# An mLSTM cell and a gated feed-forward layer: two batches of attention at a time from the third chunk on, the PSUM pool of the products split, half of the new states beside the values

## The chip, the cores and the metric

The kernel runs on one core of one Trainium2 chip. The time is the device time of one execution, in microseconds (us). A core has a matrix engine (TensorE, PE in the profile, its weight loads PEld), a vector engine (VectorE, DVE), a scalar engine (ScalarE, ACT), GpSimd (POOL) and SyncE (SP), which issues the transfers here. Each engine takes its own queue of instructions in order and waits on semaphores for the others. Results of TensorE go to PSUM, which has 8 banks; everything else works from SBUF.

## What is computed

For 4 batches and 8 heads, over 768 time steps with 40 elements per head, the reference runs a recurrent cell and feeds its output to a feed-forward layer, all in float32:

```python
for t in range(S):
    m_new = np.maximum(f_gate[:, :, t] + m, i_gate[:, :, t])
    f_stab = np.exp(f_gate[:, :, t] + m - m_new)
    i_stab = np.exp(i_gate[:, :, t] - m_new)
    m = m_new
    C = f_stab[:, :, None, None] * C + i_stab[:, :, None, None] * np.einsum('bhd,bhe->bhde', vt, kt)
    n = f_stab[:, :, None] * n + i_stab[:, :, None] * kt
    h_tilde = np.einsum('bhde,bhe->bhd', C, qt)
    nq = np.einsum('bhd,bhd->bh', n, qt)[:, :, None]
    denom = np.maximum(np.abs(nq), 1.0)
    y[:, :, t] = 1.0 / (1.0 + np.exp(-o_gate[:, :, t])) * h_tilde / denom
x = y as (batch*time, head*40)              # 3072 x 320
h = x @ w_in                                # 320 -> 2048
out = (h * (1.0 / (1.0 + np.exp(-1.702 * h)))) @ w_out   # 2048 -> 320
```

## The kernel before

**Tiling.** Time is cut into six chunks of 128 steps (chunk 0 to 5, `w` in the code). Within a chunk the recurrence becomes attention: a 128x128 matrix of weights per head from the gates, times the scores of queries and keys, times the values, plus the queries times the state that the chunks before left. At the end of a chunk the state (one 40x41 block per head) is scaled and the chunk's own sum is added. A chunk has 4 batches x 128 steps = 512 tokens, which are the columns of the feed-forward layer.

**Functions, one per step.** `columns` transposes the gate sums to columns (`p_cols`). `weights(w, b)` turns batch `b`'s row of gate sums into weights: eight exponentials on ScalarE (line 330), then a mask on GpSimd (line 333). `scores(w, b)` makes eight 40-row products of queries and keys in two PSUM tiles (`p_s`, line 343) and multiplies them into the weights on VectorE (two instructions at line 345). `values(w, b)` makes the products with the values (`p_o`, line 354) and with the state (`p_i`, line 360), then VectorE runs a chain of seven instructions (lines 364 to 374) that ends in `y`, and GpSimd copies a 64-column tail of it (line 376). `seam(w, b)` transposes `y` on TensorE (`p_x`, line 383); ScalarE copies it to `xT`. `scale(w, b)` scales the values and the old state on GpSimd (lines 390 and 394). `carry(w)` makes the chunk's sums in two halves of 16 heads (`p_c`, line 403) and adds them to the state on VectorE (line 407). `transposes(w, b)` transposes queries and keys on VectorE (line 298).

`up(w, j, n)` is the first layer (`p_h`, lines 429 and 435) with the activation on ScalarE (line 440). The second layer is `down` for chunk 0 (four accumulators of 320 columns, 16 blocks), and `down_fast` for the others: 14 blocks of eight matmuls (`p_out`, line 530), seven for each pair of batches, in a scheme that needs seven products in place of eight and sums of hidden columns and of weights (`hidden_sums`, lines 511 to 515, on VectorE). Behind each block, VectorE copies or adds its accumulator into the output tile (lines 533 and 535); blocks 5 and 6, and 12 and 13, end with the store of one batch's rows.

**Order.** The order on each engine is the order of the calls (a manual schedule); semaphores follow from tiles and pools. Chunk w+1's attention is laid among chunk w's down blocks: `attention(w + 1)` returns a list of steps, and behind each block whose number is in `stops` the next step is run. Before, a step holds one function each of up to four batches: the weights of batch s, the scores of batch s-1, the values of s-2, the seam of s-3. `carry` runs early in the next chunk's `up`.

**PSUM.** Two pools of four banks: `ps_a` (tag "a": columns, scores, values, states, seams, and half of an `up`'s hidden tiles) and `ps_m` (tag "m": the other half of the hidden tiles and all `p_out`). A tile takes the next bank of its pool in turn; its first matmul waits until what was in the bank has been read.

```python
elif w + 2 < NW and i == 0:
    load_gates(w + 2)
    load_blocks(w + 2)
block()
if i in stops and side:
    run(side.pop(0))
```

Of the kernel before, what the change touches and what calls it, by code (L numbers as in the profile page):

```python
# [8 lines left out]
FP = mybir.dt.float32  # L9
# [5 lines left out]
PSUM = bass.MemoryType.PSUM  # L15
# [7 lines left out]
L = 128  # L23
# [11 lines left out]
def kernel(  # L35
# [13 lines left out]
    B, H, S, D = q.shape  # L49
    BH = B * H  # L50
    DM = H * D
    DFF = moe_w_in.shape[1]
    NW = S // L
    NP = H // 2
    NF = DFF // 128
    D1 = D + 1
# [12 lines left out]
    op = ctx.enter_context(tc.tile_pool(name="op", bufs=2))  # L69
    rows = ctx.enter_context(tc.tile_pool(name="rows", bufs=2, space=bass.MemoryType.DRAM))  # L70
    ps_a = ctx.enter_context(tc.tile_pool(name="ps_a", bufs=4, space=PSUM))
    ps_m = ctx.enter_context(tc.tile_pool(name="ps_m", bufs=4, space=PSUM))
    ctx.enter_context(tc.manual_schedule())

    V, A, G, T = nc.vector, nc.scalar, nc.gpsimd, nc.tensor
# [9 lines left out]
    v_st = const.tile([L, BH, D1], FP, name="v_st")  # L85
# [130 lines left out]
    kT, qT, wt, ys, xT, gs, o_ps, sums = {}, {}, {}, {}, {}, {}, {}, {}  # L216
# [119 lines left out]
            A.activation(out=eo[w], in_=eo[w], func=AF.Tanh, scale=0.5)  # L336

    def scores(w, b):
        pw = [ps_a.tile([L, NP, L], FP, tag="a", name="p_s") for _ in range(2)]
        for p in range(NP):  # L340
            for i in range(2):
                r = slice(i * 64, i * 64 + D)
                T.matmul(pw[i][:, p, :], kT[w, b][r, p, :], qT[w, b][r, p, :], start=True, stop=True)  # L343
        for i in range(2):
            V.tensor_tensor(out=wt[w, b][:, :, i, :], in0=pw[i], in1=wt[w, b][:, :, i, :], op=OP.mult)  # L345
# [47 lines left out]
            old = state[:, b * NP:(b + 1) * NP].rearrange("p j a b -> p j (a b)")  # L393
            G.tensor_tensor(out=old, in0=old, in1=d, op=OP.mult)

    def carry(w):
        for c in range(2):
            ps = slice(c * 2 * NP, (c + 1) * 2 * NP)
            pc = ps_a.tile([128, 2 * NP, D1], FP, tag="a", name="p_c")
            for p in range(2 * NP):  # L400
                for i in range(2):
                    h = c * 4 * NP + 2 * p + i
                    T.matmul(pc[i * 64:i * 64 + D, p, :], k_st[:, h, 0:D], v_st[:, h, :], start=True, stop=True)  # L403
            for i in range(2):
                r = slice(i * 64, i * 64 + D)
                if w:
                    V.tensor_tensor(out=state[r, ps, i, :], in0=pc[r], in1=state[r, ps, i, :], op=OP.add)
                else:
                    V.tensor_copy(out=state[r, ps, i, :], in_=pc[r])
        G.memset(v_st[:, :, D:D1], 1.0)  # L410


    def up(w, j, n, between=None, states=False):

        x = xT[w].rearrange("p c b t -> p c (b t)")
        begin, end = range(j, j + n // 2), range(j + n // 2, j + n)
        ph = {}
        ts = slice(0, W)  # L420

        def take(j, pool, tag):
            ph[j] = [pool.tile([128, W], FP, tag=tag, name="p_h") for _ in range(2)]

        def full(j, first):
            for c in range(2):
                for i in range(2):
                    f = 2 * j + i
                    T.matmul(ph[j][i][:, ts], w_in_sb[:, c, f * 128:(f + 1) * 128], x[:, c, ts],  # L429
                             start=(first and c == 0), stop=(not first and c == 1))  # L430

        def rest(j, first):
            for i in range(2):
                r = slice(i * 64, i * 64 + 64)
                T.matmul(ph[j][i][:, ts], w_in_x[r, j, :], x[r, 2, ts], start=first, stop=not first)  # L435

        def gelu(j):
            g = gs[w, j] = gp.tile([128, 2, W], FP, tag="g", name="g")
            for i in range(2):
                A.activation(out=g[:, i, :], in_=ph[j][i], func=AF.Gelu_apprx_sigmoid)  # L440

        if between:
            for k in (j, j + 1):
                take(k, ps_m, "m")
            ts = slice(0, W // 2)
            full(j, True)
            between[0]()
            rest(j, False)
            rest(j + 1, True)
            between[1]()  # L450
            full(j + 1, False)
            between[2]()
            ts = slice(W // 2, W)
        for k in begin:
            if k not in ph:
                take(k, ps_m, "m")
            full(k, True)
        if states:
            carry(w)
        for k in begin:  # L460
            rest(k, False)
            gelu(k)
        for k in end:
            if k not in ph:
                take(k, *((ps_m, "m") if n == 2 else (ps_a, "a")))
            rest(k, True)
        for k in end:
            full(k, False)
            gelu(k)

    def down(w, b, n):
        if n == 0:
            o_ps[w, b] = ps_m.tile([128, DM], FP, tag="m", name="p_out")
        po = o_ps[w, b]
        for f in range(n * 4, n * 4 + 4):
            T.matmul(po, gs[w, f // 2][:, f % 2, b * L:(b + 1) * L], w_out_sb[:, f, :], start=(f == 0),  # L476
                     stop=(f == NF - 1))
        if n == NF // 4 - 1:
            o = op.tile([128, DM], FP, tag="o", name="o_sb")
            V.tensor_copy(out=o, in_=po)  # L480
            nc.sync.dma_start(out=out[b * S + w * L:b * S + (w + 1) * L, :], in_=o)
# [68 lines left out]


    def attention(w):
        steps = [[(columns, w)]]
        for s in range(B + 3):
            step = []
            for lag, f in ((3, seam), (2, values), (1, scores), (0, weights)):
                if 0 <= s - lag < B:
                    step.append((f, w, s - lag))
            if 0 <= s - 2 < B and w + 1 < NW:
                step.append((scale, w, s - 2))  # L560
            steps.append(step)
        return steps
# [55 lines left out]
    for w in range(NW):  # L618
        more = w + 1 < NW
        for j in range(NF // 2):  # L620
            if j % 2 == 0:
                if w:
                    if j % 4 == 0:
                        up(w, j, 4, states=more and j == 0)
                elif j == 0:
                    up(w, j, 2, (lambda: values(0, 2), lambda: values(0, 3),
                                 lambda: (seam(0, 2), seam(0, 3), convert(3), convert(4))))
                    for b in range(B):
                        scale(0, b)
                    weights_in(0)  # L630
                else:
                    weights_in(j // 2)
                    up(w, j, 2, states=(j == 2))
            if j == 0 and more:
                load(w + 1, "o")
            if w == 0 and j == 0:
                gates(1)
                load_blocks(1, 0)
                spread(1)
            if w == 1 and j == 1:  # L640
                weight_sums()
            if more:
                if w and j == 0:
                    gates(w + 1)
                if j == 4:
                    if w == 0:
                        load_blocks(1, 1)
                    load(w + 1, "v")
                    if w:
                        spread(w + 1)  # L650
                if j == (4 if w else 6):
                    load(w + 1, "k")
                if w == 0 and j == 0:
                    G.memset(q_bl, 0.0)
                if w and 4 <= j < 6:
                    transposes(w + 1, 2 * j - 8)
                    transposes(w + 1, 2 * j - 7)
            if w and j >= 4:
                hidden_sums(w, (j - 4,), False)
                if j % 2:  # L660
                    hidden_sums(w, (j - 5, j - 4), True)
        side = attention(w + 1) if more else []
        if w == 0:

            blocks = [(lambda b=b, n=n: down(w, b, n)) for ns in ((0, 1), (2,), (3,)) for b in range(B) for n in ns]
            stops = (0, 1, 5, 7, 9, 11, 13, 15)
        else:
            blocks = down_fast(w, 0) + down_fast(w, 1)
            stops = (0, 1, 2, 4, 6, 8, 10, 12)
        for i, block in enumerate(blocks):  # L670
            if w == 0:
                weights_in(4 + i)
                for b in {2: (0, 1), 8: (2,), 10: (3,)}.get(i, ()):
                    transposes(1, b)
            elif w + 2 < NW and i == 0:
                load_gates(w + 2)
# [4 lines that stand above are left out]
        if w == 0:  # L681
            load_gates(2)
            load_blocks(2)
# [30 lines left out]
```

## Time and profile before

Five runs took 511.5 us in the median (510.2 to 512.69). The profiled execution took 511.5 us; its span, from the first instruction to the last, is 509.8 us.

| what | us | of the span |
|---|---|---|
| TensorE busy | 499.2 | 98% |
| TensorE weight loads (beside it) | 353.2 | 69% |
| VectorE busy | 264.9 | 52% |
| ScalarE busy | 168.1 | 33% |
| GpSimd busy | 68.2 | 13% |
| first layer, `p_h` (lines 429, 435), in the chain that ended last | | 40% |
| second layer, `p_out` (lines 530, 476), in that chain | | 36% |
| `p_o`, `p_s`, `p_i`, `p_c`, `p_x` together, in that chain | | 12.8% |

Chunk 0 fills the first 119 us (its attention, the conversion of the feed-forward weights on VectorE and ScalarE, its up and down projection with chunk 1's attention). Each of chunks 1 to 4 takes some 80 us, and chunk 5, which has no attention beside it, the rest. A matmul in float32 shows as two records, so a `p_out` block of eight has x16, a batch's `p_s` x16, `p_o` x32, `p_i` x16. The granted clock is 1.0 of full speed. A matmul's start is when it begins to read; neighbouring matmuls overlap, so the length of a group is read from its start to the start of the next group.

### The profile page before, as it was taken

What the parts mean: (1) busy time and instruction counts of PE and PEld (TensorE: products, weight loads), DVE (VectorE), ACT (ScalarE), POOL (GpSimd) and SP (SyncE); (2) the same over time, 40 slices, a digit from 0 to 9 for tenths busy, and PEclk for the clock granted to TensorE, in tenths of its full rate; (3) what the DMA queues carried; (4) which work ended last, traced back from release to release, by engine and by line L of the source; (5) the groups of instructions that cost most, each with busy time, mean ns of one, the idle gap of its engine ahead of it and who ended that gap; (6) DMA issues with size and microseconds to landing.
All of it is one profiled execution on the core that took longest, in us unless ns stands there. A gap on an engine that the chain in (4) does not pass through costs nothing.

```text
span 509.8 us, 9498 instructions
## 1 busy us (share of the span) xinstructions
PE 499.2 (98%) x3838; PEld 353.2 (69%) x3838; DVE 264.9 (52%) x579; ACT 168.1 (33%) x373; POOL 68.2 (13%) x109
## 2 busy tenths in 40 slices
PE   8899999999999999999999999999999999999997
PEld 5774457775448998446999445999644899744797
DVE  6879984972857452519444317465144745202511
ACT  5556766301326301224521113720132730132100
POOL 7240001321000231000322000141100111000000
DMA  9999699104699502595400394600485000000000
GB/s 149 172 304 298 89 256 183 15 27 71 69 272 96 81 1 61 85 205 59 47 27 14 68 260 51 64 28 1 79 206 64 0 28 2 27 0 0 1 27 26
DMA packets 175691, 44.80 MB, mean 88 GB/s; under 512 B 164352, under 2 KB 170528, under 8 KB 175648
## 3 DMA queue, kind: packets, MB, share of 16 engines
q1 hardware_dynamic: 175648, 44.21, 46.0%
q8 instruction: 30, 0.49, 0.4%
q14 instruction: 13, 0.11, 0.1%
HBM read 40.17 MB, written 4.01 MB: 87 GB/s over the span
## 4 chain that ended last, share of the span: by engine, by line
PE 90%; DVE 6%; POOL 1%; issue 1%; ACT 1%; DVEq 0%; POOLq 0%
PE p_h L429 32%; PE p_out L530 31%; PE p_h L435 8%; PE p_out L476 5%; PE p_o L354 4%; PE p_s L343 4%; PE p_i L360 2%; PE p_c L403 1%; PE p_x L383 1%; DVE wt L345 1%; DVE w_in_sb L229 1%; DVE w_out_sb L231 0%; DVE w_in_sb L231 0%; DVE w_in_sb L228 0%; ACT xT L384 0%
## 5 line engine op out<-in xcount | busy, mean ns | idle before, releaser
L429 PE MATMUL p_h<-xT,w_in_sb 128*128 128x512 f32 (+1 forms) x400 | 170.7, 580 | 2.1 <-ACT xT L384 1.2
L429 PEld LDWEIGHTS p_h<-xT,w_in_sb 128*128 128x128 f32 x400 | 74.2, 190 | 93.1 <-issue 88.4
L440 ACT ACTIVATE g<-p_h 128x512 f32<-128x512 f32 x96 | 53.5, 599 | 151.7 <-PE p_h L435 85.3
L530 PE MATMUL p_out<-w_out_sb,g 128*128 128x160 f32 x480 | 71.3, 302 | 0.0
L530 PEld LDWEIGHTS p_out<-w_out_sb,g 128*128 128x128 f32 x480 | 66.8, 190 | 3.7 <-issue 2.4
L535 DVE TENSOR_TENSOR o_sb<-o_sb,p_out 128x160 f32<-128x160 f32 x70 | 21.4, 318 | 72.2 <-PE p_out L530 71.7
L384 ACT COPY xT<-p_x 128x384 f32<-128x384 f32 x24 | 11.4, 479 | 135.0 <-PE p_x L383 135.0
L514 DVE TENSOR_TENSOR s<-g 128x512 f32<-128x512 f32 x20 | 13.6, 681 | 75.9 <-ACT g L440 75.9
L333 POOL TENSOR_SCALAR_AFFINE_SELECT wt<-wt 128x1024 f32<-128x1024 f32 x24 | 26.6, 1109 | 184.8 <-ACT wt L330 146.8
L330 ACT ACTIVATE wt<-wt,cols 128x128 f32<-128x128 f32 x160 | 48.4, 391 | 0.0
L530 PE MATMUL p_out<-t,s 128*128 128x160 f32 x320 | 47.4, 301 | 0.0
L435 PE MATMUL p_h<-xT,w_in_x 64*128 64x512 f32 (+1 forms) x200 | 45.3, 588 | 0.2 <-DVE w_in_x L233 0.2
L530 PEld LDWEIGHTS p_out<-t,s 128*128 128x128 f32 x320 | 44.3, 190 | 0.5
L476 PE MATMUL p_out<-w_out_sb,g 128*128 128x320 f32 x128 | 36.2, 437 | 0.0
L345 DVE TENSOR_TENSOR wt<-p_s,wt 128x512 f32<-128x512 f32 x48 | 30.8, 682 | 8.1 <-PE p_s L343 5.3
L435 PEld LDWEIGHTS p_h<-xT,w_in_x 64*128 64x128 f32 x200 | 18.1, 186 | 22.6 <-issue 18.8
L476 PEld LDWEIGHTS p_out<-w_out_sb,g 128*128 128x128 f32 x128 | 23.8, 190 | 10.1 <-issue 0.5
L343 PE MATMUL p_s<-qT,kT 40*128 40x128 f32 x384 | 27.9, 284 | 1.7 <-DVE qT L298 1.3
L354 PEld LDWEIGHTS p_o<-v_st,wt 128*64 128x64 f32 x768 | 24.3, 138 | 6.4 <-issue 4.6
L354 PE MATMUL p_o<-v_st,wt 128*64 128x41 f32 x768 | 27.2, 231 | 1.4 <-DVE wt L345 1.4
L343 PEld LDWEIGHTS p_s<-qT,kT 40*128 40x128 f32 x384 | 23.4, 187 | 5.3 <-PE p_i L360 1.6
L364 DVE TENSOR_TENSOR u<-p_i,cols 128x328 f32<-128x328 f32 x20 | 9.9, 495 | 28.5 <-PE p_i L360 28.5
(117 smaller groups left out, 501.6 us busy)
## 6 DMA issues: line engine op xcount, KB each, us to landing
wt<-m_row SPq DMA_DIRECT2D x20, 512.0 KB, 6.1
bits<-in_moe_w_in_dram SPq DMA_DIRECT2D x8, 512.0 KB, 5.8
out_dram<-o_sb SPq DMA_DIRECT2D x24, 160.0 KB, 1.8
eo<-in_o_gate_dram SPq DMA_DIRECT2D x5, 640.0 KB, 5.9
v_st<-in_v_dram SPq DMA_DIRECT2D x5, 640.0 KB, 5.7
k_st<-in_k_dram SPq DMA_DIRECT2D x5, 640.0 KB, 10.9
bits<-in_moe_w_out_dram SPq DMA_DIRECT2D x8, 320.0 KB, 4.5
k_bl<-in_k_dram SPq DMA_DIRECT2D x40, 64.0 KB, 2.6
```

Of the source, the lines that this page charges most:

```text
L330: A.activation(out=x[:, h, :], in_=x[:, h, :], func=AF.Exp, scale=-1.0, bias=cols[w][:, b * H + h:b * H + h + 1])
L333: G.affine_select(out=x, in_=x, compare_op=OP.is_ge, fill=0.0, base=0, pattern=[[0, H], [1, L]], channel_multiplier=-1)
L343: T.matmul(pw[i][:, p, :], kT[w, b][r, p, :], qT[w, b][r, p, :], start=True, stop=True)
L345: V.tensor_tensor(out=wt[w, b][:, :, i, :], in0=pw[i], in1=wt[w, b][:, :, i, :], op=OP.mult)
L354: T.matmul(po[t, h, :], wt[w, b][:, p, i, t], v_st[:, b * H + h, :], start=True, stop=True)
L429: T.matmul(ph[j][i][:, ts], w_in_sb[:, c, f * 128:(f + 1) * 128], x[:, c, ts], start=(first and c == 0), stop=(not first and c == 1))
L435: T.matmul(ph[j][i][:, ts], w_in_x[r, j, :], x[r, 2, ts], start=first, stop=not first)
L440: A.activation(out=g[:, i, :], in_=ph[j][i], func=AF.Gelu_apprx_sigmoid)
L476: T.matmul(po, gs[w, f // 2][:, f % 2, b * L:(b + 1) * L], w_out_sb[:, f, :], start=(f == 0), stop=(f == NF - 1))
L514: V.tensor_tensor(out=s1, in0=a10, in1=a11, op=OP.add)
L530: T.matmul(po, a(f), b[:, f, :], start=(f == 0), stop=(f == NH - 1))
L535: V.tensor_tensor(out=dst, in0=x, in1=po, op=OP.add)
```

## The change

- In `attention`, from chunk 2 on, the batches go in pairs: weights 0 and 1; scores 0 and 1 with weights 2 and 3; values 0 and 1, then scores 2 and 3, then the scalings of 0 and 1; seams 0 and 1, values 2 and 3, then the first half of `carry` and the scalings of 2 and 3; seam 2; seam 3. Chunk 1's attention keeps its steps.
- The stops for the 14 blocks become 0, 1, 2, 4, 8, 11, 12.
- `carry` takes the halves it shall do. For chunks 2 to 4 the first half is in the attention, and `up` does the second.
- `ps_m` has two banks in place of four, and a new pool `ps_x` has two. `p_out` of chunks 1 to 5 has `ps_m` alone. The hidden tiles that had four banks of `ps_m` have two of each; chunk 0's four accumulators likewise. Scores of even batches from chunk 2 on move from `ps_a` to `ps_x`.
- During chunk 0's down projection, chunk 1's transposes of batches 2 and 3 are called ahead of blocks 7 and 9, where they were ahead of blocks 8 and 10.

```diff
-    ps_m = ctx.enter_context(tc.tile_pool(name="ps_m", bufs=4, space=PSUM))
+    ps_m = ctx.enter_context(tc.tile_pool(name="ps_m", bufs=2, space=PSUM))
+    ps_x = ctx.enter_context(tc.tile_pool(name="ps_x", bufs=2, space=PSUM))
...
     def scores(w, b):
-        pw = [ps_a.tile([L, NP, L], FP, tag="a", name="p_s") for _ in range(2)]
+        pool, tag = (ps_x, "x") if w > 1 and b % 2 == 0 else (ps_a, "a")
+        pw = [pool.tile([L, NP, L], FP, tag=tag, name="p_s") for _ in range(2)]
...
-    def carry(w):
-        for c in range(2):
+    def carry(w, cs=range(2)):
+        for c in cs:
...
-        G.memset(v_st[:, :, D:D1], 1.0)
+        if 1 in cs:
+            G.memset(v_st[:, :, D:D1], 1.0)
...
         for k in begin:
             if k not in ph:
-                take(k, ps_m, "m")
+                take(k, *((ps_m, "m") if k == j else (ps_x, "x")))
             full(k, True)
         if states:
-            carry(w)
+            carry(w, range(2) if w < 2 else (1,))
...
-            o_ps[w, b] = ps_m.tile([128, DM], FP, tag="m", name="p_out")
+            o_ps[w, b] = (ps_m if b < 2 else ps_x).tile([128, DM], FP, tag="mx"[b // 2], name="p_out")
...
     def attention(w):
+        if w > 1:
+            return [[(columns, w)], [(weights, w, 0), (weights, w, 1)],
+                    [(scores, w, 0), (scores, w, 1), (weights, w, 2), (weights, w, 3)],
+                    [(values, w, 0), (values, w, 1), (scores, w, 2), (scores, w, 3)] +
+                    [(scale, w, b) for b in (0, 1) if w + 1 < NW],
+                    [(seam, w, 0), (seam, w, 1), (values, w, 2), (values, w, 3)] +
+                    ([(carry, w, (0,)), (scale, w, 2), (scale, w, 3)] if w + 1 < NW else []),
+                    [(seam, w, 2)], [(seam, w, 3)]]
...
-            stops = (0, 1, 2, 4, 6, 8, 10, 12)
+            stops = (0, 1, 2, 4, 8, 11, 12)
...
-                for b in {2: (0, 1), 8: (2,), 10: (3,)}.get(i, ()):
+                for b in {2: (0, 1), 7: (2,), 9: (3,)}.get(i, ()):
                     transposes(1, b)
```

More of the change, by code (lines that the diff above doesn't have):

```diff
@@ L442, in up @@
         if between:
-            for k in (j, j + 1):
-                take(k, ps_m, "m")
+            take(j, ps_m, "m")
+            take(j + 1, ps_x, "x")
             ts = slice(0, W // 2)
@@ L455, in up @@
             if k not in ph:
-                take(k, ps_m, "m")
+                take(k, *((ps_m, "m") if k == j else (ps_x, "x")))
             full(k, True)
         if states:
-            carry(w)
+            carry(w, range(2) if w < 2 else (1,))
         for k in begin:
@@ L464, in up @@
             if k not in ph:
-                take(k, *((ps_m, "m") if n == 2 else (ps_a, "a")))
+                take(k, *((ps_x, "x") if n == 2 else (ps_a, "a")))
             rest(k, True)
@@ L558, in attention @@
                     step.append((f, w, s - lag))
-            if 0 <= s - 2 < B and w + 1 < NW:
+            if 0 <= s - 2 < B:
                 step.append((scale, w, s - 2))
```

## The prediction

> **What bounds the kernel now.** I read the page first (busy shares, then the chain that ended last), then the waits, then single instructions in order of time on TensorE and VectorE.
>
> ```profile
> PE 499.2 (98%) x3838; PEld 353.2 (69%) x3838; DVE 264.9 (52%) x579; ACT 168.1 (33%) x373; POOL 68.2 (13%) x109
> ...
> PE 90%; DVE 6%; POOL 1%; issue 1%; ACT 1%; DVEq 0%; POOLq 0%
> ```
>
> TensorE is busy for 98% of the span and carries 90% of the chain; and in order of time none of its idle gaps lies behind 119.1 us. So time can be won there in two ways only: take away one of its few waits, or make its own work shorter. The first of those, in chunk 1's attention (columns here and below: start us, us, engine, line, operation, count, idle before it and what ended it):
>
> ```profile
> 96.27 0.77 PE L360 MATMUL p_i<-state,qT 128*64 128x82 f32 x16
> 97.89 1.16 PE L343 MATMUL p_s<-qT,kT 40*128 40x128 f32 x16 [0.84 <-DVE qT L298]
> ...
> 104.77 0.77 PE L360 MATMUL p_i<-state,qT 128*64 128x82 f32 x16
> 106.01 1.16 PE L343 MATMUL p_s<-qT,kT 40*128 40x128 f32 x16 [0.47 <-DVE qT L298]
> ```
>
> From chunk 2 on there are no gaps, but the starts show what a change of matmul shape costs:
>
> ```profile
> 163.69 2.44 PE L530 MATMUL p_out<-t,s 128*128 128x160 f32 x16
> 165.97 2.34 PE L530 MATMUL p_out<-w_out_sb,g 128*128 128x160 f32 x16
> 168.23 1.13 PE L354 MATMUL p_o<-v_st,wt 128*64 128x41 f32 x32
> 169.19 0.77 PE L360 MATMUL p_i<-state,qT 128*64 128x82 f32 x16
> 169.89 1.16 PE L343 MATMUL p_s<-qT,kT 40*128 40x128 f32 x16
> 170.98 2.44 PE L530 MATMUL p_out<-t,g 128*128 128x160 f32 x16
> ...
> 175.43 0.49 PE L383 MATMUL p_x<-ident,y 128*128 128x128 f32 x3
> 175.85 1.13 PE L354 MATMUL p_o<-v_st,wt 128*64 128x41 f32 x32
> ...
> 197.19 0.49 PE L383 MATMUL p_x<-ident,y 128*128 128x128 f32 x3
> 197.52 2.34 PE L530 MATMUL p_out<-w_out_sb,s 128*128 128x160 f32 x16
> ```
>
> A p_out block between its like takes 2.17 us from start to start (476.21, 478.38, 480.56 in the last down projection). Behind p_s it takes 2.28 (163.69 to 165.97), ahead of p_o 2.26; p_x takes 0.42 ahead of p_o (175.43 to 175.85) and 0.33 ahead of p_out.
>
> VectorE has room on average, but not at each point:
>
> ```profile
> 159.62 0.68 DVE L512 TENSOR_TENSOR s<-g,s 128x512 f32<-128x512 f32 x1
> 160.33 0.32 DVE L533 COPY o_sb<-p_out 128x160 f32<-128x160 f32 x1
> ...
> 170.00 0.50 DVE L364 TENSOR_TENSOR u<-p_i,cols 128x328 f32<-128x328 f32 x1 [1.34 <-PE p_i L360]
> ...
> 172.48 1.28 DVE L345 TENSOR_TENSOR wt<-p_s,wt 128x512 f32<-128x512 f32 x2
> 173.68 0.31 DVE L535 TENSOR_TENSOR o_sb<-o_sb,p_out 128x160 f32<-128x160 f32 x1
> ```
>
> Block 0 of the down projection ended at 157.82, yet its copy starts at 160.33, behind the hidden sums. A values chain takes 2.48 us (170.00 to 172.48), two score products 1.20 (172.48 to 173.68).
>
> **The change part by part.** The profiled execution took 511.5 us (span 509.8, 1.7 around it), which is also the median of the five runs; the sum is made against 511.5.
>
> *Chunk 1's transposes one block earlier.* The two waits above go. p_i to p_s took 1.62 and 1.24 us where 0.70 is undisturbed (169.19 to 169.89): 0.92 + 0.54 = 1.46 us. Batch 2's pair (1.27 us) moves into VectorE's idle 2.46 us before 89.51; batch 3's pair takes the place that batch 2's had, so batch 1's chain starts at 97.67 as before. Next late would be batch 2's chain: VectorE is free at 104.56, the matmuls deliver at 104.66. **-1.46.** Without that cover the chain, not TensorE, would wait; the worst is the 1.46 given back.
>
> *Two batches together (four down stages, chunks 1 to 4).* TensorE's shapes in a stage ran full, s, full, o, s, full, o, s, full, o, s, full, o, full (full is p_out and p_x, s is p_s, o is p_o and p_i): 13 switches. Now it is full, s, full, o, s, full, o, full: 7. Gone are two of each of three kinds. s to full: the last p_s pair is 0.09 longer than the 0.11 that pairs are apart, and the block behind it 0.10: 0.19. Full to o: 0.09, and 0.02 on the first p_o pair: 0.12. o to s: p_i's last pair 0.09, p_s's first 0.10: 0.19. 2 x 0.50 = 1.0 us, by unrounded starts 1.02. p_o to p_i starts 0.05 after, no switch, and p_i to the next p_o is the same shape. **-4.08 in four stages.** Were p_i to p_o a switch (0.19, two in each stage), 1.5 us of it would be lost.
>
> *Half the state products beside the values (three stages).* The 32 p_c records cost 0.65 us wherever they run (64 of them 1.36 in the chain, entering included). Unseen is p_i to p_c: between 0 (as p_o to p_i) and 0.19 (the dearest switch). I take 0, as both write half-width tiles; 3 x 0.19 = 0.57 is kept for the range. The Trainium skill, "TensorEngine Tiling (Array Packing)", Key Properties, says that a change of tiling mode drains the engine, and lists no 40-column mode under its 64-column one; by it the price is 0, else the total would be 0.6 higher. k_st, which it needs 19 us earlier, landed at 158.29 for a use near 187.
>
> *Two buffers for p_out instead of four.* Block 2 now waits for block 0's copy. Block 2 started at 160.33, the copy ends at 160.65; a VectorE end reaches TensorE after 0.05 (the chain: products end at 16.80, p_o starts at 16.84) to 0.15 (transpose end 97.74, p_s 97.89). I take 0.05, the row that also reads PSUM: 0.38 us. The same from the other stages' starts: 0.38, 0.38, and 0.60, 0.60 in the last two, where block 2 starts earlier against the copy (401.72 against 401.94, 480.56 against 480.78). **+2.34** (2.8 with 0.15). The hidden sums end when the gelus do, so they don't move away.
>
> *VectorE's queue in the merged stretch.* Both values chains and four products now lie before block 5's addition, which block 7 needs. From batch 0's first p_i: 0.81 until VectorE starts (169.19 to 170.00), 2 x 2.48, 2 x 1.20, 0.32, 0.05 = 8.54. TensorE meanwhile: 0.61 (p_i without the switch behind it) + 0.93 (p_o without the one ahead) + 0.70 + 1.98 (two p_s in one) + 2.28 + 2.17 = 8.67. Hidden, with 0.13 to spare. Likewise block 9's addition, behind two chains and two state additions (207.59 to 208.62), which block 11 needs: 0.81 + 4.96 + 1.03 + 0.32 + 0.05 = 7.17 against 0.61 + 0.93 + 0.61 + 0.74 (half of p_c and its switch) + 2.28 + 2.17 = 7.34. **0**, the thinnest cover here; a miss costs its size, seven times.
>
> *Moved work, at nothing.* Batch 1's products wait for its mask (POOL until 167.08), with block 3's additions queued behind them; those are needed by block 5 near 175. Masks 2 and 3 come earlier, behind ACT's exponentials. POOL's scalings of two batches (2.9 us) end near 180, p_c needs them at 187. ACT's four xT copies (0.48) have a block behind the last. SP: two stores follow within a block, 1.8 us to land, and block 7's copy may wait some tenths for its output buffer; block 9 needs it two blocks and the whole of values 2 and 3 later.
>
> Sum: 511.5 - 1.46 - 4.08 + 2.34 = **508.3**.
>
> **The rivals.**
> 1. *The thin covers miss.* Four misses at block 7 and three at block 11 of 0.3 us: +2.1, 510.4. For: margins of 0.13 and 0.17. Against: every term is a start-to-start time, stable to 0.01 over the stages.
> 2. *POOL slows VectorE (the slower side).* POOL's scalings now run beside the four products. In chunk 1 an instruction of VectorE stretched beside them:
>
> ```profile
> 85.53 0.69 DVE L231 SCALAR_TENSOR_TENSOR w_out_sb<-bits,w_out_sb 128x512 uint32<-128x512 uint32 x1
> ...
> 94.59 1.10 DVE L231 SCALAR_TENSOR_TENSOR w_out_sb<-bits,w_out_sb 128x512 uint32<-128x512 uint32 x1
> ```
>
>    At 1.10/0.69 the products grow from 2.40 to 3.8 us, at L229's 0.84/0.43 to 4.7; less 0.13, block 7 waits 1.3 to 2.2 us in the three stages that have scalings: 512.1 to 514.8. It turns the gain into a loss from 1.07 us a stage. Against it: the addition at 188.92, which like the products reads PSUM and one SBUF tile, took 0.31 beside POOL's scaling of 188.82. "SBUF — State Buffer", Who interferes with whom, of the Trainium skill says the same of instructions with one SBUF input and the opposite of two; by it products stay at 2.40.
> 3. *The switches don't go.* Should a batch boundary cost what a switch did, only 1.46 is won and 2.34 lost: 512.4. Against: p_o to p_i above.
> 4. *No wait at block 2*, if copies or sums run sooner than I think: 506.0. Little speaks for it.
>
> **How the numbers follow.** My case 0.64; rivals 1 to 4: 0.16, 0.11, 0.05, 0.04. About 0.3% (1.5 us) can be told from no change, so faster means below 510.0. My case's own range is 507.6 (pieces of stall smaller) to 509.4 (p_c switch 0.57, release at 0.15). Faster: 0.64 + 0.04 and 0.02 of rival 1 (smaller misses), 0.70; same: the other 0.14 of it, rival 3, and 0.02 from the low end of rival 2, 0.21; slower: the rest of rival 2, 0.09. The range reaches from 507.3, just below my case's own, to 511.6, past rival 1; rivals 2, 3 and 4, 0.20 together, are left out.
>
> **What would show it.** A wait of 0.3 to 0.6 us of p_out on VectorE's copy in each of five down stages; no wait of p_s on qT near 97 and 106; p_s x32 near 1.98 us; p_i to p_c within 0.07; no waits at blocks 7 and 11. I am wrong if those two show waits, if score products beside POOL take over 0.75 us, or if p_i to p_o takes 0.15 or more.

## The result and the profile after

The changed kernel takes 509.09 us in the median of 26 runs (507.68 to 512.88), the kernel before 511.59 in 47 (510.18 to 515.5). The ratio is 0.9952, 95% interval 0.9939 to 0.9965: 2.5 us faster, where 3.2 were forecast (508.3).

One thing has to be known before the traces are compared. Most runs of both kernels lie in two clusters of times, 1.4 us apart: 510.2 and 511.6 before, 507.7 and 509.1 after. The profile of before is of the upper cluster, that of after (507.69 us, span 506.0) of the lower. Both medians fall in the upper cluster, and within a cluster the gain is 2.5 us in both. The difference between clusters arises between 34 and 69 us, and is taken up at the end.

The page after:

```profile
PE 495.2 (98%) x3838; PEld 351.7 (70%) x3838; DVE 263.5 (52%) x579; ACT 167.6 (33%) x373; POOL 68.8 (14%) x109
...
PE 89%; DVE 6%; POOL 1%; ACT 1%; issue 1%; DVEq 0%; POOLq 0%
```

TensorE is still the bound. Its waits have changed (engine, line, what it waited for: us in total, times, longest):

```profile
PE p_out L533 <- DVE o_sb L536: 1.5, 5, 0.4
PE p_o L356 <- DVE wt L347: 1.4, 1, 1.4
PE p_h L432 <- ACT xT L386: 1.2, 2, 0.6
```

The waits of `p_s` on `qT` are gone; one wait of `p_out` on the copy of block 0 has come in each of five down projections. In order of time, the down projection of chunk 1 on TensorE, then on VectorE (start, us, engine, line, operation, idle before it):

```profile
155.31 2.42 PE L533 MATMUL p_out<-t,s 128*128 128x160 f32 x16
157.95 2.44 PE L533 MATMUL p_out<-w_out_sb,g 128*128 128x160 f32 x16 [0.22 <-DVE o_sb L536]
160.32 2.06 PE L345 MATMUL p_s<-qT,kT 40*128 40x128 f32 x32
...
167.80 0.77 PE L362 MATMUL p_i<-state,qT 128*64 128x82 f32 x16
168.40 1.08 PE L356 MATMUL p_o<-v_st,wt 128*64 128x41 f32 x32
...
176.44 2.34 PE L533 MATMUL p_out<-w_out_sb,g 128*128 128x160 f32 x16
...
183.99 0.77 PE L362 MATMUL p_i<-state,qT 128*64 128x82 f32 x16
184.60 0.78 PE L405 MATMUL p_c<-v_st,k_st 128*40 128x41 f32 x32
185.31 2.44 PE L533 MATMUL p_out<-w_out_sb,g 128*128 128x160 f32 x16
187.58 2.34 PE L533 MATMUL p_out<-t,s 128*128 128x160 f32 x16
189.81 2.44 PE L533 MATMUL p_out<-w_out_sb,g 128*128 128x160 f32 x16
192.08 0.49 PE L385 MATMUL p_x<-ident,y 128*128 128x128 f32 x3
```

```profile
157.57 0.33 DVE L536 COPY o_sb<-p_out 128x160 f32<-128x160 f32 x1
...
173.57 2.48 DVE L347 TENSOR_TENSOR wt<-p_s,wt 128x512 f32<-128x512 f32 x4
175.96 0.31 DVE L538 TENSOR_TENSOR o_sb<-o_sb,p_out 128x160 f32<-128x160 f32 x1
...
183.31 0.50 DVE L366 TENSOR_TENSOR u<-p_i,cols 128x328 f32<-128x328 f32 x1 [2.00 <-PE p_i L362]
...
188.40 1.00 DVE L409 TENSOR_TENSOR state<-p_c,state 40x328 f32<-40x328 f32 x2
189.43 0.32 DVE L538 TENSOR_TENSOR o_sb<-o_sb,p_out 128x160 f32<-128x160 f32 x1
```

By starts of stages, the change of 2.5 us divides so: chunk 0's down projection 50.26 to 48.81 us (-1.45); the down projections of chunks 1, 2 and 3 with the first layer behind each, 80.54 to 80.08 (-0.46 each); chunk 4 with its first layer 78.96 to 78.58 (-0.38); chunk 5's down projection, which has no attention beside it, 33.58 to 34.29 (+0.71). The sum is -2.50.

### The profile page after: what moved, and what is told of

It is laid out like the page before. It is cut to its first block, busy times and chain, and to the rows that moved or that the text cites. A ratio compares the mean times of both kernels' runs of the same rounds, so it can differ in the third digit from the quotient of the medians.

```text
span 506.0 us, 9501 instructions
## 1 busy us (share of the span) xinstructions
PE 495.2 (98%) x3838; PEld 351.7 (70%) x3838; DVE 263.5 (52%) x579; ACT 167.6 (33%) x373; POOL 68.8 (14%) x109
## 4 chain that ended last, share of the span: by engine, by line
PE 89%; DVE 6%; POOL 1%; ACT 1%; issue 1%; DVEq 0%; POOLq 0%
PE p_h L432 33%; PE p_out L533 27%; PE p_h L438 9%; PE p_out L479 7%; PE p_o L356 5%; PE p_s L345 4%; PE p_i L362 2%; PE p_x L385 1%; PE p_c L405 1%; DVE s L515 1%; DVE g L514 1%; DVE s L517 1%; DVE s L518 1%; ACT g L443 1%; DVE wt L347 0%
## 5 line engine op out<-in xcount | busy, mean ns | idle before, releaser
L345 PE MATMUL p_s<-qT,kT 40*128 40x128 f32 x384 | 25.8, 280 | 0.4 <-DVE wt L347 0.4
L409 DVE TENSOR_TENSOR state<-p_c,state 40x328 f32<-40x328 f32 x16 | 7.9, 496 | 30.6 <-PE p_c L405 30.5
```

## The experiments

**The earlier transposes alone.**

```diff
-                for b in {2: (0, 1), 8: (2,), 10: (3,)}.get(i, ()):
+                for b in {2: (0, 1), 7: (2,), 9: (3,)}.get(i, ()):
```

> The kernel before with the two transposes called ahead of blocks 7 and 9, nothing else. My theory: both waits of p_s on qT go, 1.44 us of the 511.6: 510.15. Rival: the conversions of the weights make batch 1's or 2's chain late in their place, and less than half is won: 510.9 or more.

Measured: 510.14 us, ratio 0.9977 (0.9961 to 0.9992); chunk 0's down projection takes 48.81 us, all other stages are as before. This step is worth 1.45 us and owes nothing to the others.

**One batch at a time, with the new pools.** The branch of `attention` for pairs goes, the stops are those of before, `carry` does both halves in `up`, and the last chunk's attention again leaves out its scalings.

```diff
-        if w > 1:
-            return [[(columns, w)], [(weights, w, 0), (weights, w, 1)],
...
-            stops = (0, 1, 2, 4, 8, 11, 12)
+            stops = (0, 1, 2, 4, 6, 8, 10, 12)
```

> The changed kernel with the steps of attention and the stops of before, and the states in the first layer: the pools split in three and the earlier transposes stay. My theory: the pairs are worth 1.09 us a stage through the six changes of matmul shape, the wait at block 2 stays as it is (2.87 us in all) and the wait at block 11 (0.46) goes: 509.1 + 4.36 - 0.46 = 513.0. Rival: the gain is from the pools or from shorter queues on VectorE, not from the shapes: 510.5 or less.

Measured: 513.03 us, ratio 1.0045 (1.0026 to 1.0064), slower than the kernel before. A down projection of chunks 1 to 4 takes 44.54 us, against 43.45 in the next run, which differs by the pairs and their stops alone (chunk 1: 154.28 to 198.82, and 154.94 to 198.39): 1.09 us a stage for six changes of shape. TensorE waits for `o_sb` 1.5 us in five waits in both runs, so the queues on VectorE do not make the difference. The new pools without the pairs are a loss.

**Both halves of the states in the first layer.**

```diff
-                    ([(carry, w, (0,)), (scale, w, 2), (scale, w, 3)] if w + 1 < NW else []),
+                    ([(scale, w, 2), (scale, w, 3)] if w + 1 < NW else []),
...
-            carry(w, range(2) if w < 2 else (1,))
+            carry(w)
```

> Both halves of the new states stay in the first layer, as before; the pairs, the pools and the transposes are as in the changed kernel. My theory: the two state additions are what makes block 9's addition late, so block 11's wait and restart (0.15 us a stage) go in three stages, and the products of the states cost the same in either place: 508.6 against 509.1. Rival: the half beside the values is a gain because it saves time in the first layer: 509.5 or more.

Measured: 508.7 us, ratio 0.9941 (0.9923 to 0.9958). Down projection and first layer together take 79.94 us a chunk instead of 80.08. The profiled execution took 509.3 us, as chunk 0's down projection has 0.6 us more in it: batch 0's scores wait for queries that landed late. The intervals of this run and of the changed kernel overlap, so that the half is a small loss there rests on the stages of the traces: block 11 no longer waits (block 10 starts at 189.04, block 11 at 191.21, and what follows it at 193.39, 2.17 us apart):

```profile
186.76 2.44 PE L533 MATMUL p_out<-w_out_sb,g 128*128 128x160 f32 x16
189.04 2.34 PE L533 MATMUL p_out<-t,s 128*128 128x160 f32 x16
191.21 2.34 PE L533 MATMUL p_out<-w_out_sb,g 128*128 128x160 f32 x16
193.39 0.49 PE L385 MATMUL p_x<-ident,y 128*128 128x128 f32 x3
```

**A third bank for block 0.** `product` may take its accumulator from `ps_x`, which is free before the first scores and after the last.

```diff
-        def product(a, b, *adds):
-            po = ps_m.tile([128, DH], FP, tag="m", name="p_out")
+        def product(a, b, *adds, x=False):
+            po = (ps_x if x else ps_m).tile([128, DH], FP, tag="x" if x else "m", name="p_out")
...
-        return [lambda: product(block(0, 0), w00, (o00, None)),
+        return [lambda: product(block(0, 0), w00, (o00, None), x=c == 0),
```

> Block 0 of each down projection puts its product into the pool ps_x, which is free at that point; all else as in the changed kernel. My theory: block 2's wait for VectorE's copy and the slow restart behind it are a matter of the second bank alone, so blocks 1 and 2 fall from 5.01 to 4.52 us in chunks 1 to 3 (5.18 to 4.47 in chunk 4, and 0.70 less in chunk 5), 2.87 us in all: 506.2 against 509.1. Rival: VectorE is behind by the hidden sums whatever the banks, and the wait moves on to block 3 or to the score products: half or less is won, 507.7 or more.

Measured: 506.24 us, ratio 0.9908 (0.9874 to 0.9943). TensorE and VectorE in the same stretch:

```profile
156.73 2.42 PE L533 MATMUL p_out<-t,s 128*128 128x160 f32 x16
158.99 2.34 PE L533 MATMUL p_out<-w_out_sb,g 128*128 128x160 f32 x16
161.25 0.94 PE L345 MATMUL p_s<-qT,kT 40*128 40x128 f32 x12
```

```profile
158.28 0.68 DVE L515 TENSOR_TENSOR s<-g,s 128x512 f32<-128x512 f32 x1
158.99 0.33 DVE L536 COPY o_sb<-p_out 128x160 f32<-128x160 f32 x1
```

The copy is as late as before, behind the hidden sums, but block 2 starts with it and not behind it. So the loss was the second bank and not VectorE's lateness in itself. Block 2 up to `p_s` takes 2.26 us here (158.99 to 161.25) and 2.37 after the wait (157.95 to 160.32): a block that has waited is 0.1 us longer as well.

**Blocks 0 and 9 there.**

```diff
-                lambda: product(block(1, 0), w01, (o10, o01)),
+                lambda: product(block(1, 0), w01, (o10, o01), x=c == 1),
```

> As the run with block 0 in ps_x, and block 9's product goes there too, so that block 11 no longer waits for its addition. My theory: 0.15 us in each of three stages on top of the 2.87: 505.8 (506.24 measured with block 0 alone). Rival: the late additions push the next bank's reader, block 12, and nothing is won: 506.2.

Measured: 505.7 us, ratio 0.987 (0.9841 to 0.9899); the down projections of chunks 1 to 3 fall from 43.73 to 43.57 us, the 0.15 expected. With it, down projection and first layer take 79.44 us a chunk. The run with all states in the first layer, with block 2's wait taken off as well, would by estimate take 79.45 (79.94 - 0.49). So by these stages where the half of the states is done makes no difference in itself.

**The two pools of before, with the pairs.**

```diff
-    ps_m = ctx.enter_context(tc.tile_pool(name="ps_m", bufs=2, space=PSUM))
-    ps_x = ctx.enter_context(tc.tile_pool(name="ps_x", bufs=2, space=PSUM))
+    ps_m = ctx.enter_context(tc.tile_pool(name="ps_m", bufs=4, space=PSUM))
...
-        pool, tag = (ps_x, "x") if w > 1 and b % 2 == 0 else (ps_a, "a")
+        pool, tag = ps_a, "a"
...
```

> The changed kernel with the two pools of four banks of before: scores of all batches in ps_a, p_out and hidden tiles in ps_m. My theory: block 2's and block 11's waits go (2.87 + 0.46), but batch 3's scores then need the bank of batch 1's p_o, which VectorE frees 3.5 us after batch 0's chain begins, 1.3 us after TensorE gets there; with the restart 1.4 us in each of four stages: 509.1 - 3.3 + 5.5 = 511.3. Rival: the split isn't needed for the pairs: 505.8.

Measured: 511.15 us, ratio 0.9979 (0.9953 to 1.0006). That this is near 511.3 is luck. The forecast is for the upper cluster. The profile (511.16 us) is of the lower one, with a shift of 0.84 us, and 1.68 us of it is a stretch of halved clock in chunk 2 that was not forecast (see the end). Two runs without such a stretch took 509.39 and 509.49 us, and one 1.4 us above them 510.82, which is what the forecast has to be held against. The wait comes where it was expected:

```profile
PE p_s L344 <- DVE u L365: 1.9, 4, 0.5
```

A stage of chunks 1 and 3 takes 44.84 us, 1.27 more than with blocks 0 and 9 in `ps_x`, where 1.4 were expected. The pairs need the split: a stage with its first layer takes 80.72 us here and 80.54 with the earlier transposes alone, so in two pools the pairs lose 0.2 us a chunk.

**Both blocks, and chunk 1's last two steps one block earlier.**

```diff
-            stops = (0, 1, 5, 7, 9, 11, 13, 15)
+            stops = (0, 1, 5, 7, 9, 11, 12, 14)
```

> Blocks 0 and 9 in ps_x, and in chunk 0's down projection the last two steps of chunk 1's attention one block earlier (behind blocks 12 and 14 instead of 13 and 15), so that a block covers the copy of the last transposed batch. My theory: the 0.57 us wait of the first layer on that copy and the 0.16 beside it go, and the chain of batch 2 is just in time: 505.1. Rival: batch 3's p_o or its transposes now wait for VectorE's chain instead: 505.8 or more.

Measured: 504.96 us, ratio 0.9857 (0.9833 to 0.9882). Chunk 0's down projection falls from 48.81 to 48.12 us. This is faster than both kernels: 6.6 us under the kernel before, 4.1 under the changed one.

**The clearing of `q_bl` moved.** This and the next run concern the two clusters.

```diff
-                if w == 0 and j == 0:
+                if w == 0 and j == 2:
                     G.memset(q_bl, 0.0)
```

> The kernel before with that clearing moved in the same way and nothing else. My theory: its slow cluster at 511.6 goes too, 510.2 in nearly all runs. Rival: both clusters stay, 510.2 and 511.6.

Measured on the kernel before: 510.25 us, eleven of twelve runs between 510.23 and 510.28, the other 510.93. The upper cluster is gone; ratio 0.9975 (0.9964 to 0.9985).

> The kernel with blocks 0 and 9 in ps_x and the earlier seam, and GpSimd's clearing of q_bl moved from behind chunk 0's first pair of hidden tiles to behind the second. My theory of the two clusters of times, 1.4 us apart, that every kernel here shows: one conversion step of VectorE (the shift, 512 elements) comes up while GpSimd scales the values, and either runs in 0.84 us between two of its instructions or, in the slow cluster, only ends with the clearing, after 2.6 us, with TensorE waiting for that piece of weights. Without the clearing there, no run is in the slow cluster: 503.6 in nearly all (505.0 was the median with it). Rival: the clusters come from the transfers or the clock, and stay: half of the runs near 505.0.

Measured: 504.26 us in four runs (503.6, 503.63, 504.89, 505.21), ratio 0.9855 (0.9833 to 0.9877). Here the expectation held only in part: two of four runs lie near 505, which is the rival's number. In the profile (504.89 us) the shift takes its 0.84 us and the first layer its 33.12, but chunk 0's down projection takes 49.43: batch 0's scores wait 1.2 us for `qT`, and its transpose, which waits for `q_bl`, starts at 81.38 us (77.84 in the profile of the changed kernel). SyncE issued the loads of `q_bl` from 67.96 us on, and from 65.10 in the changed kernel. Moving the clearing need not be the reason: with the clearing in its old place, the run with both halves of the states in the first layer issued them from 69.03 us on and waited as well. Why they were issued later was not settled.

## Why the prediction was right, and where it was off

The direction, the mechanism of the main parts and the range held. The gain was 0.7 us smaller than the sum: the pairs won 0.28 us more, the waits at block 2 cost 0.5 more, and those at block 11 cost 0.46 that were put at nothing. The prediction named a wait at block 11 as a sign of being wrong, and there it was. It knew nothing of the two clusters: that both medians fell in the same one was luck.

- **Transposes, -1.46.** Measured -1.45. The cover was there: in the trace after, `p_i` to `p_s` takes 0.70 us twice (94.96 to 95.66, 102.54 to 103.24):

```profile
94.96 0.77 PE L362 MATMUL p_i<-state,qT 128*64 128x82 f32 x16
95.66 1.16 PE L345 MATMUL p_s<-qT,kT 40*128 40x128 f32 x16
```

- **Pairs, -4.08.** Measured 1.09 a stage, -4.36. Adding up single switches was right; a `p_o` group behind `p_i` was 0.90 and not 0.93.
- **Half of the states, 0.** `p_i` to `p_c` takes 0.60 (183.99 to 184.60), the same as `p_i` to `p_o`: no switch. The Trainium skill's "TensorEngine Tiling (Array Packing)", Key Properties, says that a change of mode, and not just of the tile, drains TensorE. The 0.60 agrees with it if `p_c` runs in the 64-column mode of `p_o`, which no run here shows.
- **Two banks, +2.34.** Here the size failed. The wait itself came as worked out: the copy ends at 157.89, block 2 starts at 157.95 instead of 157.57, 0.38 late, with 0.05 from VectorE's end to TensorE's start. What the sum lacked is that the block is then some 0.11 longer. By the stages, the waits and these losses make 2.87 in the five down projections, and the run with a third bank took 2.85 off.
- **VectorE's queue at block 7, hidden.** Right by a hair, as said: the addition ends at 176.27, with 0.05 to reach TensorE, and block 7 starts on time at 176.44. The four products took 2.39 us beside POOL's scalings (173.57 to 175.96, against 2.40 assumed), so rival 2 falls. The Trainium skill's "SBUF — State Buffer", Who interferes with whom, agrees: by it an instruction of VectorE with at most one SBUF input, outside the two-port modes, does not contend with GpSimd. Two of the scalings beside the products:

```profile
173.91 0.74 POOL L392 TENSOR_TENSOR v_st<-v_st,cols 128x328 f32<-128x328 f32 x1
174.60 0.73 POOL L396 TENSOR_TENSOR state<-state,cols 128x328 f32<-128x328 f32 x1
```

- **VectorE's queue at block 11, hidden.** This step failed, and rival 1 came true in this half. 7.17 us were forecast from batch 2's first `p_i` to TensorE's start; it was 7.31 (182.49 to 189.81). The chains of batches 2 and 3 took 2.55 and 2.54 us instead of 2.48 (183.31, 185.86, 188.40): the last of their instructions, which writes `y`, starts some 0.07 later than in batch 0's. Two chains make 0.14, which is the whole miss of VectorE's side. The trace shows what differs: ahead of this write, in batches 2 and 3 of all four chunks, VectorE runs an instruction that only waits on a semaphore (185.38), and the write itself waits on GpSimd's, which it does for no other batch and nowhere in the kernel before. GpSimd's copy of the tail, which uses the same buffer two batches earlier, had long ended (171.24, 0.24 us). So the likely cause is that in the new order nothing VectorE has waited for before covers that copy; no run takes this wait away. TensorE got there earlier than thought, at 189.76, so block 11 waited 0.05 and then lost another 0.1. In three stages 0.46.

So the sum by measured terms is -1.45 - 4.36 + 2.87 + 0.46 = -2.48, against -2.50 by the stages.

Rival 3 (the switches stay) fell with the run of single batches, rival 4 (no wait at block 2) with the profile. The 26 runs cannot tell 508.3 from 509.1 by themselves, as their clusters are wider apart than that; the stages can.

## What to carry to other kernels

Where TensorE is never idle, as here, time can still be won by grouping its matmuls by shape (1.09 us for six switches): read starts of neighbouring groups, not busy times, and count switches. A pool that loses banks for it must be checked at the point where the engine that empties it is furthest behind, here right behind the hidden sums, and a bank that is free at just that moment cost nothing here. Margins of 0.1 to 0.2 us on a chain of some twenty instructions are thin: the one of 0.13 held and the one of 0.17 did not, as a new order can add waits on semaphores that cost time even where they are long fulfilled. The price of a miss is more than the wait (0.05 waited, 0.15 lost).

## What was not expected of the hardware

**The end of a wait costs 0.1 us.** In the profile after, each of the eight blocks of `p_out` that had waited for their bank ran 0.1 us longer than the same block without the wait (2.37 against 2.26 ahead of `p_s`, 2.28 against 2.17 ahead of `p_x` or another block). It is what a block also loses behind a change of shape (2.28 against 2.17).

**Two clusters from one VectorE instruction.** In chunk 0, a shift of the weight conversion comes up while GpSimd scales the values. Before (upper cluster), on GpSimd and VectorE:

```profile
33.12 3.00 POOL L390 TENSOR_TENSOR v_st<-v_st,cols 128x328 f32<-128x328 f32 x4
36.06 1.80 POOL L654 MEMSET q_bl<- 128x2048 f32 x1
```

```profile
35.56 2.58 DVE L229 TENSOR_SCALAR w_in_sb<-w_in_sb 128x512 uint32<-128x512 uint32 x1
```

After (lower cluster):

```profile
36.14 2.08 POOL L666 MEMSET q_bl<- 128x2048 f32 x1
```

```profile
35.64 0.84 DVE L230 TENSOR_SCALAR w_in_sb<-w_in_sb 128x512 uint32<-128x512 uint32 x1
```

A shift like it takes 0.43 us alone (40.06 before). In the one case the shift ends 0.28 us behind GpSimd's clearing (38.14, 37.86); in the other it ends first (36.48), and the clearing takes 0.28 longer. The Trainium skill's "SBUF — State Buffer", Who interferes with whom, says that where VectorE runs in a two-port mode, whichever of the two engines issues first gets the shared ports for its whole instruction and the other blocks. These numbers agree if the order is settled when a scaling ends, since the shift starts ahead of the clearing in both profiles; no run shows the ports. That it makes the clusters is shown for the kernel before by moving the clearing. The other profiles fit: all five others with the long shift (2.58 or 2.59 us) are of the upper cluster. In the kernel with both blocks and the earlier seam, a second wait of about the same size, on `q_bl`, appeared in its place in one profile.

**A halved clock behind a short wait.** In the profile with two pools, chunk 2's down projection took 46.52 us and the same stage of chunks 1 and 3 44.84. The wait ends at 251.91 us, and from 253.8 us on the granted clock (the column after the engines) was halved for 3.4 us:

```profile
252.00:254.00 2.00, 1.95 (x19) 1.64 (x20) 1.86 (x7) 0.00 (x0) 0.03 (x1) 0.95 0.00 0
254.00:256.00 2.00, 2.00 (x9) 2.00 (x9) 2.00 (x4) 0.00 (x0) 2.00 (x4) 0.50 0.00 0
256.00:258.00 2.00, 2.00 (x12) 2.00 (x11) 0.62 (x2) 0.00 (x0) 0.99 (x2) 0.70 0.03 8
```

Six of this kernel's ten runs have the same mean clock as this one, 0.997, and none of the changed kernel's 26 (four of those have 0.990 to 0.993). But the same wait in the other three stages didn't do it, so that the wait was the cause was not shown.
